# The attention's gate setup is reordered: triangle ahead of identity copies, factors behind one scan, spreads by unit, an own buffer for suffix products, and position stores at other steps

## The chip, the cores and the metric

The kernel runs on one core of one Trainium2 chip. The metric is the device time of one execution in microseconds. TensorE is the matmul engine (PE), VectorE is DVE, ScalarE is ACT, GpSimd is POOL, and SP issues most DMAs. "Unit" below is one step of the attention's main loop.

## The reference

Three stages run one after the other. The first is a gated linear attention over 4 batches, 8 heads, 768 tokens and a head width of 40, with a running maximum m over the gates:

    m_new  = max(f_gate + m, i_gate)
    f_stab = exp(f_gate + m - m_new);  i_stab = exp(i_gate - m_new)
    C = f_stab * C + i_stab * outer(v, k);  n = f_stab * n + i_stab * k
    y = sigmoid(o_gate) * (C q) / max(|n q|, 1)

The second sends each of the 3072 tokens (320 wide) to one of 8 experts by the largest cosine logit; an expert is two matrices with a relu of width 1024, and its result is scaled by the softmax weight. The third is one dense block of width 2048 with x * sigmoid(1.702 x).

## The kernel before

**Attention.** The tokens are cut into 6 chunks of 128. A unit is one (batch, chunk) pair, the batch running fastest, so there are 24 units, and units 0 to 3 are chunk 0. Inside a chunk the products of f_stab between two tokens form a 128 x 128 decay matrix for each head (`pm`). Chunk 0 makes it in `scan0`: matmuls with the identity spread the gates over the partitions (L452) and two VectorE scans turn them into products (L454). Chunks from 1 on make two 64 x 64 blocks by one scan with reset points (`scan`, L430; data `fb`, read back from DRAM where `put_dec` stored it, and `id2`, which is the identity repeated for each head). The block between the halves comes from one matmul (`far_mm`, L439) of `lhsA` and `rhsB`. These are the factors `fa` (products from a token to the end of its first half, made on GpSimd by six doubling steps in `suffix`, L346) and `fb` (products from the start of the second half, the scan `est` of `gates_e`, L330), each split into a rounded part (`fp32r`, a cast on ScalarE) and a rest (a subtraction on GpSimd), and then spread over batches and heads with 0/1 masks (`spread_a`, `spread_b` on ScalarE, with `bmask` and `hmask`).

Around it a unit has the scores (`scores_mm`, L477), wm = scores x decay on VectorE (`scores_w`, L482), wm times values (`pv`, L540), the state of the chunk (`kweigh` L468 on GpSimd, `state` L491, `state_up`, on ScalarE for chunk 0, L508, else on VectorE, L512), the part that comes from earlier chunks (`inter`), the division (`epilogue1`, `epilogue2`, `finish`), and transposes and logits for the experts (`route_t`, `route_l`, L615 to L617, with `enT` from `prep_en`). `vprime` (L461) weighs the values, on GpSimd from unit 1 on.

**Opening.** Six loads bring the gates, three copies of each. Chunk 0's gates go first through `gates_m` (a scan, L302), `gates_x` (L307, L308), `gates_xi` (L312) and two exponentials (L316), then the other 640 tokens through the same, with `gates_xi` on GpSimd. `patterns` (L242 on) needs the triangle `tri`, which GpSimd makes (L218 to L220) behind the copies into `id2` (L211). The suffix products lie in the buffer `mm` of the running maxima, of which `gates_x` and `gates_xi` are readers.

**What sets the order.** Everything in the attention stands under a manual schedule: each engine takes its instructions in the order in which the program writes them, and waits in that order. The main loop is written out by hand with conditions on u; loads for unit u + 3 are issued by SP in unit u. The accumulator `dC` of the state has one buffer, so the state of a unit waits until the update of the unit before has read it.

**Experts.** Eight experts of eight steps each (`s` from 0 to 63, M1 = 8). `rows_and_gates` computes, a few VectorE instructions a step, each token's position and weight; `meta_put` (L1354) then writes for 128 tokens one (token, weight) pair each, 8 bytes, with an indirect DMA from GpSimd. There are 24 such stores; the list `puts` holds their steps. GpSimd also makes a part of the split of the expert weights (L111). The weights of the third stage (`load_c`, L1303) are loaded and converted (`cvt`, L1285 on) beside the experts.

Of the kernel before, what the change touches and what calls it, by code (L numbers as in the profile page):

```python
# [9 lines left out]
F32 = mybir.dt.float32  # L10
# [16 lines left out]
def kernel(ctx, tc, qT_in, kT_in, kvo_in, i_gate, f_gate, expert_emb, tau, w12, wio, out, dbg=None):  # L27
# [116 lines left out]
    with ExitStack() as actx:  # L144
# [65 lines left out]
        for a in range(2):  # L210
            nc.gpsimd.tensor_copy(id2[a * HP:(a + 1) * HP],  # L211
                                  ident[a * HP:(a + 1) * HP, a * HP:(a + 1) * HP].unsqueeze(1).to_broadcast([HP, H, HP]))
        fac = {n: ap1.tile([R3, NCH - CH, HP], F32R, name=n) for n in ("fa", "fb")}
# [58 lines left out]
        est = fd  # L272
        facA = mm[:, 0:(NCH - CH) * HP].rearrange("k (c t) -> k c t", t=HP)
        fz = fg.rearrange("k (c t) -> k c t", t=P)
# [39 lines left out]
        def gates_exp(t, c0, c1):  # L314
            v = rows_of(c0, c1)
            nc.scalar.activation(out=v(t), in_=v(t), func=AF.Exp)  # L316
# [22 lines left out]
        def suffix():  # L339
# [4 lines left out]
            while k < HP:  # L344
                yield
                nc.gpsimd.tensor_tensor(out=facA[:, :, 0:HP - k], in0=facA[:, :, 0:HP - k], in1=facA[:, :, k:HP], op=ALU.mult)  # L346
                k *= 2

        def factor_a(c0, c1):
            cs = slice(c0 - CH, c1 - CH)  # L350
            nc.scalar.copy(fac["fa"][:, cs], facA[:, cs])
            lo = slice(BH, 2 * BH)
            nc.gpsimd.tensor_tensor(out=fac["fa"][lo, cs], in0=facA[lo, cs], in1=fac["fa"][lo, cs].bitcast(F32), op=ALU.subtract)

        def factor_b(c0, c1):

            cs = slice(c0 - CH, c1 - CH)
            late = est[:, c0:c1, HP:P]
            nc.scalar.copy(fac["fb"][:, cs], late)
            lo = slice(2 * BH, R3)  # L360
            nc.gpsimd.tensor_tensor(out=fac["fb"][lo, cs], in0=late[lo], in1=fac["fb"][lo, cs].bitcast(F32), op=ALU.subtract)
            n = c1 - c0
            nc.gpsimd.tensor_tensor(out=late, in0=late, in1=est[:, c0:c1, HP - 1:HP].to_broadcast([R3, n, HP]), op=ALU.mult)
            gd = wk.tile([BH, n, B * G], F32, tag="gd", name="gd", bufs=1)
            gd_t[c0] = gd
            nc.gpsimd.tensor_tensor(out=gd, in0=pairm.unsqueeze(1).to_broadcast([BH, n, B * G]),
                                    in1=est[0:BH, c0:c1, P - 1:P].to_broadcast([BH, n, B * G]), op=ALU.mult)

        def spread_a(c0, c1):
            cs = slice(c0 - CH, c1 - CH)  # L370
            for b in range(B):
                nc.scalar.mul(lhsA[:, b, cs], fac["fa"][:, cs].bitcast(F32), bmask[:, b:b + 1])

# [496 lines left out]
        with tc.manual_schedule():  # L870
# [17 lines left out]
            gates_x(1, NCH)  # L888
            gates_xi(1, NCH)
            gates_exp(fg, 1, NCH)  # L890
            suffix_ops = suffix()
            next(suffix_ops)
            gates_exp(ig, 1, NCH)
            masks()
            nc.sync.dma_start(out=emb, in_=expert_emb)
# [9 lines left out]
            scores_mm(0)  # L905
            gates_pe0()
            scores_w(0)
            vprime(0, nc.vector)
            gates_z(1, NCH)
            put_dec()  # L910
# [5 lines left out]
            for u in range(0, NU - 1):  # L916
# [12 lines left out]
                if ok(u - 1):  # L929
                    epilogue1(u - 1)  # L930
                if u == 1:
                    state(0)
                    scores_w(1)
                    state_up(0)
                if u in (2, 3):
                    scores_w(u)
                if u and ok(u + 1):
                    scan(u + 1)
                if u == 1:
                    gates_e(1, NCH)  # L940
                    factor_b(1, NCH)
                if u > 3:
# [3 lines left out]
                if u == 0:  # L946
                    scan(1)
                if ok(u - 1):
                    pv(u - 1)
                    if batch:  # L950
                        route_rank(batch)
                    epilogue2(u - 1)
# [6 lines left out]
                if ok(u + 1):  # L959
                    vprime(u + 1)  # L960
                    if u == 0:
                        for _ in suffix_ops:
                            pass
                    if units[u + 1][1] < CH:
                        kweigh(u + 1)
                rts = {2: [], 3: [0], 4: [1], 5: [2], 6: [3, 4]}.get(u, [u - 2] if ok(u - 2) else [])
                if rts:
# [9 lines left out]
                if u:  # L977
                    state(u)
                if u == 3:
                    prep_en()  # L980
                if len(rts) > 1:
# [18 lines left out]
                if u == 0:  # L1000
                    factor_a(1, NCH)
                    spread_a(1, NCH)
                if u in (1, 2):
                    spread_b(1, NCH, (u - 1) * H // 2, u * H // 2)
                for i in range(0 if u < US else 1 if u < NU - 5 else 2):
                    if pend:
                        scatter(pend.pop(0))
# [89 lines left out]
    with ExitStack() as mctx:  # L1097
# [427 lines left out]
        with tc.manual_schedule():  # L1525
# [33 lines left out]
            meta_ops = rows_and_gates()  # L1559
            puts = [M1 + 5 + i for i in range(M1)] + [2 * M1 + 6 + 2 * i for i in range(NTILE - M1)]  # L1560

# [14 lines left out]
            for e, m, s in steps:  # L1576
# [7 lines left out]
                if 1 <= s < 4:  # L1584
                    prep_x0(0, s - 1)
                for _ in range({2: 2, 3: 2, 4: 1, 5: 2, 6: 2}.get(s, int(6 < s < 13))):
                    next(meta_ops, None)
# [134 lines left out]
```

## Time and profile before

| | us |
|---|---|
| median of 3 runs (lowest to highest) | 746.87 (744.79 to 747.55) |
| the profiled execution | 746.67 |
| its span, first to last instruction | 744.9 |

| engine | busy, share of the span |
|---|---|
| TensorE | 97% |
| TensorE weight loads | 90% |
| VectorE | 69% |
| ScalarE | 49% |
| GpSimd | 32% |

The attention fills about the first 180 us. In the timeline each line gives the start, the duration, the engine, the line of the program and the tiles (out<-in); in brackets stands how long the engine idled just before and what ended it. Several instructions of one kind in a row are merged (x6), and the duration then covers them all. A line of the windows gives the stretch, its length, the busy us of PE, PEld, DVE, ACT and POOL (with the count of instructions), TensorE's granted clock as a share of 2.4 GHz, the busy share of the DMA engines and GB/s. The mean granted clock of TensorE over the span is 0.991 of 2.4 GHz.

### The profile page before, as it was taken

Reading aid. Unit: us, or ns where it says so; the run is one execution under the profiler, and the core shown is the slowest. Engines: PE = TensorE matmul, PEld = TensorE weight load, DVE = VectorE, ACT = ScalarE, POOL = GpSimd, SP = SyncE. Lnnn points to the kernel's source line nnn. Section 1 sums busy time; section 2 is a strip of 40 time slices with the busy share of each in tenths; the row PEclk is TensorE's granted clock in tenths of the full one; section 3 lists DMA queues with packets and bytes.
Section 4 is the critical chain, followed back from the end, with each engine's and each line's share of the span. In section 5 each row is a group of like instructions: output and inputs, shape, how many; then the busy total and the mean of one; then the engine's idle time right before and its main releaser. Section 6 shows DMA issues by size and latency. Waiting matters only on the chain.

```text
span 744.9 us, 13413 instructions
## 1 busy us (share of the span) xinstructions
PE 719.1 (97%) x4767; PEld 672.5 (90%) x4767; DVE 515.2 (69%) x1080; ACT 367.1 (49%) x855; POOL 237.9 (32%) x355
## 2 busy tenths in 40 slices
PE   7899999999999999999999999999999999999994
PEld 5899999988989899999999989888889999889994
DVE  8668999996699799999967755545545544445542
ACT  3465466545666556676645433433333333334442
POOL 6555677776224434545310003003003003002011
PEclk9899999999999999999999999999999999999998
DMA  5688888833775966777722212202201201101000
GB/s 168 183 260 268 241 243 247 263 123 107 245 273 145 214 210 191 203 196 244 227 81 72 39 37 57 63 1 58 64 1 46 54 1 43 38 0 53 6 19 18
DMA packets 70106, 93.14 MB, mean 125 GB/s; under 512 B 31858, under 2 KB 56530, under 8 KB 70034
## 3 DMA queue, kind: packets, MB, share of 16 engines
q1 hardware_dynamic: 66818, 84.05, 38.8%
q0 software_dynamic: 3072, 7.89, 3.1%
q8 instruction: 38, 0.62, 0.4%
q10 hardware_dynamic: 144, 0.30, 0.1%
q14 instruction: 34, 0.28, 0.1%
HBM read 71.11 MB, written 17.18 MB: 119 GB/s over the span
## 4 chain that ended last, share of the span: by engine, by line
issue 43%; PE 16%; DVE 6%; POOL 5%; DMA 3%; ACT 1%; POOLq 0%; SPq 0%; ACTq 0%; DVEq 0%
PE acc L1221 8%; PE hp L139 7%; POOL out_dram L1266 3%; DMA c<-in_wio_dram 2%; POOL xr L1377 2%; DVE hs L1195 1%; DVE w L122 1%; PE xt L1145 1%; DVE w L112 1%; DMA xr<-y 1%; DVE ex L1287 1%; DVE xl L1147 1%; DVE ex L1292 1%; DVE wout L122 0%; DVE fr L1290 0%
## 5 line engine op out<-in xcount | busy, mean ns | idle before, releaser
L1221 PE MATMUL acc<-wout,hhl 128*128 128x320 f32 x1152 | 187.3, 309 | 0.0
L1221 PEld LDWEIGHTS acc<-wout,hhl 128*128 128x128 f32 x1152 | 175.9, 188 | 7.8 <-DVE o L1248 0.2
L1206 DVE TENSOR_TENSOR sg<-hp,sg 128x512 f32<-128x512 f32 (+1 forms) x112 | 68.9, 615 | 93.4 <-ACT sg L1205 85.8
L139 PE MATMUL hp<-xh,win 128*128 128x512 f32 (+1 forms) x560 | 131.0, 364 | 0.0
L1266 POOL DMA_INDIRECT out_dram<-o,tokd x24 | 24.0, 1002 | 312.7 <-ACT o L1250 309.0
L1205 ACT ACTIVATE sg<-hp 128x512 f32<-128x512 f32 (+1 forms) x112 | 60.4, 539 | 125.0 <-PE hp L139 124.5
L1208 DVE TENSOR_TENSOR hhl<-sg,hhl 128x512 fp32r<-128x512 f32 (+1 forms) x112 | 71.4, 637 | 70.3 <-ACT hhl L1207 69.8
L1221 PE MATMUL acc<-w,hs 128*128 128x320 f32 x636 | 105.0, 310 | 2.7 <-ACT hs L1194 1.4
L139 PEld LDWEIGHTS hp<-xh,win 128*128 128x128 f32 x560 | 93.9, 188 | 11.5 <-ACT xh L1416 0.2
L1207 ACT CAST hhl<-sg 128x512 fp32r<-128x512 f32 (+1 forms) x112 | 62.7, 560 | 80.1 <-DVE sg L1206 77.1
L1221 PEld LDWEIGHTS acc<-w,hs 128*128 128x128 f32 x636 | 96.6, 188 | 5.5 <-DVE hs L1195 2.0
L139 PE MATMUL hp<-xl,win 128*128 128x512 f32 (+1 forms) x336 | 85.7, 363 | 0.0
L111 POOL TENSOR_TENSOR w<-r,w 128x256 fp32r<-128x256 f32 x58 | 49.5, 853 | 102.5 <-ACT w L106 78.9
L139 PEld LDWEIGHTS hp<-xl,win 128*128 128x128 f32 x336 | 58.9, 189 | 10.9 <-DVE xl L1417 0.2
L139 PE MATMUL hp<-xh,w 128*128 128x440 f32 (+6 forms) x320 | 66.8, 338 | 0.0
L139 PEld LDWEIGHTS hp<-xh,w 128*128 128x128 f32 x320 | 51.4, 189 | 1.7
L477 PE MATMUL sp<-qT,kblk 120*128 120x128 f32 x384 | 48.8, 282 | 0.2 <-DVE wm L482 0.2
L1194 ACT ACTIVATE hs<-hp 128x440 fp32r<-128x440 f32 (+6 forms) x64 | 30.2, 471 | 34.8 <-PE hp L139 32.0
L477 PEld LDWEIGHTS sp<-qT,kblk 120*128 120x128 f32 x384 | 46.5, 198 | 0.9 <-issue 0.5
L540 PE MATMUL op<-vp_in,wm 128*128 128x96 f32 (+1 forms) x368 | 43.6, 272 | 0.0
L540 PEld LDWEIGHTS op<-vp_in,wm 128*128 128x128 f32 x368 | 42.9, 192 | 0.0
L139 PE MATMUL hp<-xl,w 128*128 128x440 f32 (+6 forms) x192 | 42.9, 331 | 0.0
(323 smaller groups left out, 1128.6 us busy)
## 6 DMA issues: line engine op xcount, KB each, us to landing
r<-in_w_dram SPq DMA_DIRECT2D x32, 704.0 KB
kvo<-in_kvo_dram SPq DMA_DIRECT2D x24, 480.0 KB
c<-in_wio_dram SPq DMA_DIRECT2D x16, 704.0 KB
fb<-dec SPq DMA_DIRECT2D x40, 128.0 KB
rows<-zt SPq DMA_DIRECT2D x8, 640.0 KB
qT<-in_qT_dram SPq DMA_DIRECT2D x24, 180.0 KB
xr<-y SPq DMA_DIRECT2D x5, 640.0 KB
kblk<-in_kT_dram SPq DMA_DIRECT2D x48, 60.0 KB
```

The lines of the kernel that those rows point to most:

```text
L111: eng.tensor_tensor(out=t[:, 3 * P:5 * P].rearrange("p (c f) -> p c f", c=2), in0=r1[:, 0:2], in1=hif[:, 0:2], op=ALU.subtract)
L139: nc.tensor.matmul(hp, a, b, start=(i == 0), stop=(i == len(seq) - 1))
L477: nc.tensor.matmul(sp[:, h - hs.start], kblk[u % NLD][0:KR, h // 3, h % 3, :], qT[u][0:KR, h // 3, :], start=True, stop=True)
L540: nc.tensor.matmul(ops[:, h * NW:h * NW + n], wm[u][:, h], vp_in[u % NLD][:, h * DV:h * DV + n], start=True, stop=True)
L1194: nc.scalar.activation(out=hh, in_=hp, func=AF.Relu)
L1205: nc.scalar.activation(out=sg, in_=hp, func=AF.Sigmoid, scale=1.702)
L1206: nc.vector.tensor_tensor(out=g, in0=hp, in1=sg, op=ALU.mult)
L1207: nc.scalar.copy(hh, g)
L1208: nc.vector.tensor_tensor(out=hl, in0=g, in1=hh.bitcast(F32), op=ALU.subtract)
L1221: nc.tensor.matmul(acc_t[blk][i], hl if j == 2 else hh, w[:, DM:2 * DM] if j == 1 else w[:, 0:DM], start=(first and j == 0), stop=(last an ...
L1266: sc = nc.gpsimd.indirect_dma_start(out=out, out_offset=bass.IndirectOffsetOnAxis(ap=tokd[:, ti:ti + 1], axis=0), in_=o[:, i], in_offset=None)
L1377: eng.tensor_tensor(out=xr_t[blk], in0=xr_t[blk], in1=gated[:, t0:t0 + n].unsqueeze(2).to_broadcast([P, n, 3 * P]), op=ALU.mult)
```

## The change

- The identity copies into `id2` go from GpSimd to ScalarE, and GpSimd's next work behind the buffers' clearing is the triangle.
- `facA`, the buffer of the suffix products, is a tile of its own instead of a part of `mm`.
- `gates_xi` of chunks 1 to 5 (GpSimd) stands behind the first step of `suffix` (its memset and copy); their second exponential stands behind `gates_pe0`, the masks behind `vprime(0)`.
- `gates_e`, the scan of est, goes from unit 1 to unit 0, behind the scan of unit 1. Both casts (`fa` and `fb`) stand behind it in `factor_hi`, at the end of unit 0. The lo parts (`factor_b`, `factor_a`, GpSimd) go to unit 1, behind `vprime` and `kweigh` of unit 2.
- `spread_a` spreads one batch a unit, in units 2 to 5, instead of all four in unit 0.
- `prep_en` goes from the end of unit 3 to its front, ahead of `scan(4)`.
- The position stores go from steps 13 to 20 and then 22, 24, ... 52 to steps 11 to 15 and then 16, 18, ... 52; the last two steps of `rows_and_gates` ahead of them move from steps 11 and 12 to 9 and 10.

```diff
@@ setup
-            nc.gpsimd.tensor_copy(id2[a * HP:(a + 1) * HP],
-                                  ident[a * HP:(a + 1) * HP, a * HP:(a + 1) * HP].unsqueeze(1).to_broadcast([HP, H, HP]))
+            nc.scalar.copy(id2[a * HP:(a + 1) * HP],
+                           ident[a * HP:(a + 1) * HP, a * HP:(a + 1) * HP].unsqueeze(1).to_broadcast([HP, H, HP]))
...
-        facA = mm[:, 0:(NCH - CH) * HP].rearrange("k (c t) -> k c t", t=HP)
+        facA = ap1.tile([R3, NCH - CH, HP], F32, name="facA")
@@ factors
+        def factor_hi(c0, c1):
+            cs = slice(c0 - CH, c1 - CH)
+            nc.scalar.copy(fac["fb"][:, cs], est[:, c0:c1, HP:P])
+            nc.scalar.copy(fac["fa"][:, cs], facA[:, cs])
...
-            nc.scalar.copy(fac["fa"][:, cs], facA[:, cs])
...
-            nc.scalar.copy(fac["fb"][:, cs], late)
...
-        def spread_a(c0, c1):
+        def spread_a(c0, c1, b):
             cs = slice(c0 - CH, c1 - CH)
-            for b in range(B):
-                nc.scalar.mul(lhsA[:, b, cs], fac["fa"][:, cs].bitcast(F32), bmask[:, b:b + 1])
+            nc.scalar.mul(lhsA[:, b, cs], fac["fa"][:, cs].bitcast(F32), bmask[:, b:b + 1])
@@ ahead of the loop
-            gates_xi(1, NCH)
             gates_exp(fg, 1, NCH)
             suffix_ops = suffix()
             next(suffix_ops)
-            gates_exp(ig, 1, NCH)
-            masks()
+            gates_xi(1, NCH)
...
             gates_pe0()
+            gates_exp(ig, 1, NCH)
             scores_w(0)
             vprime(0, nc.vector)
+            masks()
@@ in the loop
+                if u == 3:
+                    prep_en()
...
-                if u == 1:
-                    gates_e(1, NCH)
-                    factor_b(1, NCH)
...
                 if u == 0:
                     scan(1)
+                    gates_e(1, NCH)
...
                     if units[u + 1][1] < CH:
                         kweigh(u + 1)
+                    if u == 1:
+                        factor_b(1, NCH)
+                        factor_a(1, NCH)
...
-                if u == 3:
-                    prep_en()
...
                 if u == 0:
-                    factor_a(1, NCH)
-                    spread_a(1, NCH)
+                    factor_hi(1, NCH)
                 if u in (1, 2):
                     spread_b(1, NCH, (u - 1) * H // 2, u * H // 2)
+                if 2 <= u < 2 + B:
+                    spread_a(1, NCH, u - 2)
@@ experts
-            puts = [M1 + 5 + i for i in range(M1)] + [2 * M1 + 6 + 2 * i for i in range(NTILE - M1)]
+            puts = [M1 + 3 + i for i in range(5)] + [2 * M1 + 2 * i for i in range(NTILE - 5)]
...
-                for _ in range({2: 2, 3: 2, 4: 1, 5: 2, 6: 2}.get(s, int(6 < s < 13))):
+                for _ in range({2: 2, 3: 2, 4: 1, 5: 2, 6: 2, 9: 2, 10: 2}.get(s, int(6 < s < 9))):
```

## Rows read from the trace of the kernel before

**Rows 1.** Page, busy time of each engine (share of the span, instructions)

```profile
PE 719.1 (97%) x4767; PEld 672.5 (90%) x4767; DVE 515.2 (69%) x1080; ACT 367.1 (49%) x855; POOL 237.9 (32%) x355
```

**Rows 2.** Windows, 70 to 75 us in the attention

```profile
70.00:75.00 5.00, 5.00 (x49) 5.00 (x48) 4.92 (x13) 2.65 (x9) 3.83 (x4) 1.00 0.93 307
```

**Rows 3.** Timeline of VectorE (start, duration), wm of units 0, 2, 5 and 21

```profile
16.37 1.23 DVE L482 TENSOR_TENSOR wm<-sp,pmb 128x1024 f32<-128x1024 f32 x1
...
31.89 1.23 DVE L482 TENSOR_TENSOR wm<-sp,pmb 128x1024 f32<-128x1024 f32 x1 [3.34 <-PE sp L477]
...
53.51 1.21 DVE L482 TENSOR_TENSOR wm<-sp,pmb 128x1024 f32<-128x1024 f32 x1
...
155.06 1.20 DVE L482 TENSOR_TENSOR wm<-sp,pmb 128x1024 f32<-128x1024 f32 x1
```

**Rows 4.** Windows of 1 us, around the fall and the rise of TensorE's clock

```profile
25.00:26.00 1.00, 0.00 (x0) 0.00 (x0) 1.00 (x1) 1.00 (x4) 0.00 (x0) 0.83 0.68 168
...
32.00:33.00 1.00, 1.00 (x9) 1.00 (x8) 1.00 (x1) 0.00 (x0) 0.72 (x1) 0.76 0.66 180
```

**Rows 5.** Timeline, all engines, 14 to 29 us: factors, state of unit 1

```profile
14.46 0.44 POOL L342 COPY mm<-fg 96x315 f32<-96x315 f32 x1 [0.61 <-DMA qT<-in_qT_dram]
...
17.72 4.75 POOL L346 TENSOR_TENSOR mm<-mm 96x315 f32<-96x315 f32 x6
...
22.51 0.46 ACT L351 CAST fa<-mm 96x320 fp32r<-96x320 f32 x1 [3.20 <-POOL mm L346]
...
24.14 1.92 ACT L372 ACTIVATE lhsA<-fa,bmask 96x320 fp32r<-96x320 f32 x4 [1.17 <-POOL fa L353]
24.65 1.46 DVE L330 TENSOR_TENSOR_SCAN fd<-fg,fd 96x640 f32<-96x640 f32 x1
...
25.96 0.84 ACT L508 ACTIVATE Cst<-dC,mask 120x123 f32<-120x123 f32 x3
...
26.95 1.42 PE L491 MATMUL dC<-vp_in,kw 128*120 128x123 f32 x6 [2.84 <-ACT Cst L508]
...
28.16 3.69 PE L477 MATMUL sp<-qT,kblk 120*128 120x128 f32 x16
```

**Rows 6.** Timeline, all engines, 5 to 14 us: the opening

```profile
5.99 0.26 DVE L242 CAST tri<-tri 128x128 bf16<-128x128 f32 x1 [1.94 <-POOL tri L220]
...
6.84 0.40 DVE L302 TENSOR_TENSOR_SCAN mm<-fg,ig 32x128 f32<-32x128 f32 x1
...
10.95 0.82 DVE L307 TENSOR_TENSOR fg<-fg,mm 96x640 f32<-96x640 f32 x1
11.00 1.95 POOL L312 TENSOR_TENSOR ig<-ig,mm 96x640 f32<-96x640 f32 x1 [3.07 <-DVE mm L302]
...
11.80 1.82 DVE L308 TENSOR_TENSOR fg<-fg,mm 96x640 f32<-96x640 f32 x1
...
13.95 2.32 DVE L454 TENSOR_TENSOR_SCAN pmb<-f,ident_h 128x512 f32<-128x512 f32 x2
```

**Rows 7.** Windows, the first 4.5 us

```profile
0.00:4.50 4.50, 2.09 (x3) 1.05 (x4) 2.82 (x13) 1.49 (x2) 3.85 (x9) 1.00 0.52 141
```

**Rows 8.** Timeline of GpSimd, values of unit 3

```profile
32.03 0.72 POOL L461 TENSOR_TENSOR vp_in<-kvo,ei_tok 128x320 f32<-128x320 f32 x1 [1.39 <-DMA kvo<-in_kvo_dram]
```

**Rows 9.** Timeline of GpSimd, values of unit 6

```profile
52.41 1.70 POOL L461 TENSOR_TENSOR vp_in<-kvo,ei_tok 128x320 f32<-128x320 f32 x1
```

**Rows 10.** Timeline of TensorE, the first logits

```profile
43.76 0.49 PE L615 MATMUL r<-enT,xT 128*128 128x128 f32 x2 [0.95 <-ACT enT L408]
```

**Rows 11.** Windows, then timeline, 235 to 260 us: position stores, a weight load

```profile
235.00:240.00 5.00, 5.00 (x32) 4.63 (x31) 4.91 (x9) 2.72 (x7) 2.79 (x4) 1.00 0.64 67
...
240.73 1.03 POOL L1354 DMA_INDIRECT meta<-metat,pos_i  x1 [0.15 <-issue]
...
256.25 0.53 DVE L1285 TENSOR_SCALAR mt<-c 128x704 int32<-128x704 int32 x1 [3.08 <-DMA c<-in_wio_dram]
...
257.59 2.02 PE L1221 MATMUL acc<-w,hs 128*128 128x320 f32 x12 [1.38 <-ACT hs L1194]
```


## The prediction

> **What bounds the kernel now.** The busy line of the page comes first: TensorE 97%, its weight loads 90%, VectorE 69% [rows 1]. That is a mean over stages, so a stretch of the attention is read next: from 70 to 75 us the weight loads fill 5.00 of 5 us and VectorE 4.92 [rows 2]. In the settled attention TensorE issues without a gap; a microsecond by which TensorE's order starts earlier should therefore reach the end. Whether it starts late is read from the product wm = scores x decay, one instruction a unit on VectorE [rows 3]. From unit 5 to unit 21 the starts lie (155.06 - 53.51) / 16 = 6.35 us apart. From unit 0 to unit 5 they need 37.14 us, where five such units are 31.75. So about 5.4 us are lost in the first units, beside what is lost ahead of unit 0. One-microsecond windows and the timeline show the hole: TensorE idles 2.84 us ahead of unit 1's state at 26.95, so from 24.11 on [rows 5]; the granted clock falls at about 25.66 (a mean of 0.83 between the levels 1 and 0.5, that is 2.4 and 1.2 GHz) and is back at about 32.5 (0.76) [rows 4].
>
> Who made TensorE wait is read backwards in the timeline [rows 5]. The state of unit 1 needs the accumulator that ScalarE's update of unit 0 empties, at 25.96. ScalarE stood before it in the cast of fa (3.20 us idle, waiting for GpSimd's suffix products, which ran 17.72 to 22.47) and in four spreads of 1.92 us (1.17 idle). The scores of unit 2 begin at 28.16 and take 3.69 us at the low clock.
>
> **Part 1, the opening.** VectorE idles 1.94 us for the triangle, which waits behind the identity copies on GpSimd [rows 6]. With the copies on ScalarE this goes, and what is next is the gate data. The six gate loads are 6 x 98,304 B = 0.59 MB; the queues had moved 141 GB/s x 4.5 us = 0.63 MB by 4.5 us [rows 7], and the first scan would start at 6.84 - 1.94 = 4.9. I take the whole 1.94 (bounds 0 and 1.94). The copies lie in ScalarE's idle time (1.49 busy of 4.5 us [rows 7]); without that cover they would cost at most the 1.94 again.
>
> The second gate subtraction took 1.82 us, its twin in front of it, of the same shape, 0.82; only GpSimd's subtraction for the other gate (1.95 us) ran beside the second throughout [rows 6]. The change moves that one behind the copy for the suffix, and the copy needs the exponential, so the two no longer meet: 1.00 us less (bounds 0 and 1.00). The masks, moved away, stood for the 0.33 us between the subtraction's end at 13.62 and the scan at 13.95. Together scan 0, and wm of unit 0 behind it, come 3.27 us earlier: 16.37 becomes 13.1. The masks then cost about 0.5 behind unit 0's values, so the store of the decays goes out some 2.7 us earlier.
>
> **Part 2, GpSimd and ScalarE.** The copy for the suffix started at 14.46 [rows 5]; 2.94 earlier is 11.5, its end 12.0, the moved subtraction (1.95 at most) ends at 13.9. That is now in front of kweigh and vprime, two products of about 0.72 [rows 8]: 15.35. Six suffix products in 4.75 end at 20.1. A new meeting must be paid: the scan of est (1.46 us, both inputs in SBUF), which stood alone at 24.65, now runs on VectorE behind scan 1, at about 18.5 to 19.9, beside these products. The price of such a meeting, by rows, is 1.82 - 0.82 = 1.00 on VectorE or 1.70 - 0.72 = 0.98 on GpSimd [rows 6, 8, 9]; I take 1.0 (bounds 0, and six times 0.98 if each product were held): 21.1.
>
> The Trainium skill states in "SBUF — State Buffer", section "Who interferes with whom", that a VectorE instruction with two SBUF inputs and a GpSimd instruction that reads SBUF block each other wholly, whichever starts second. By that rule est's scan would hold GpSimd up to its full 1.46, and the sum below would be 0.5 us poorer; the trace agrees in kind, with about 1.0 in both rows just given.
>
> Behind the suffix ScalarE casts fa (0.46); the cast of fb lies in the wait. What is queued behind that wait is the state update of unit 0 and the copy of its numerator; TensorE waits for the first. It starts at 21.6 for 25.96: 4.4 us earlier. TensorE's state of unit 1 and the scores of unit 2 follow by the same 4.4. If the clock stays up over the gap that is left, these scores need 1.95 us (their length at the high clock, as 3.69 at half is 1.85 to 1.95) for 3.69: 1.7 more. Wm of unit 2 comes at about 31.89 - 6.1 = 25.8.
>
> The lo parts of the factors now stand behind vprime and kweigh of unit 2 on GpSimd: three products more, 2.2 us, and four spreads at 0.48 behind them end near 27.3. ScalarE's next state update begins there; TensorE comes to the state that needs it only after scores, decay broadcasts and values of unit 2, near 30. This costs nothing, and 1:1 beyond about 2.5 us of delay. The four spreads of fa, 1.92 in one piece, become one of 0.48 in each of units 2 to 5, ahead of a copy that TensorE reads much later; ScalarE has room (2.65 busy of 5 us [rows 2]): 0, bounds 0 and 1.9.
>
> **Part 3, the embedding's transposes.** TensorE waited 0.95 us for their copies right before the first logits [rows 10]. Moved ahead of unit 3's scan, they are ready long before: 0.95 less (bounds 0 and 0.95; they now wait for VectorE's normalising of the embedding, which ends about a microsecond ahead of them).
>
> **Part 4, the position stores.** A window with few other transfers, 235 to 240 us, has the DMA engines 0.64 busy at 67 GB/s; at the rate of rows 2 (307 GB/s for 0.93) 67 would take 0.20, so some 0.44 x 5 = 2.2 us went to the two stores in flight, about 1.1 each [rows 2, 11]. A weight load had four stores beside it in its flight (the first is shown, at 240.73; they follow every 2 to 4 us); VectorE waited 3.08 us for it and TensorE then 1.38 [rows 11]. With steps 16 and 18 alone there are two fewer. Bounds 0 and 1.38; I take 0.5, since one late operand can replace the other. The two small vector instructions pulled two steps ahead are the same work: 0, bounds 0.4 either way.
>
> **Sum.** 6.1 + 0.95 + 0.5 = 7.55 us against the profiled execution's 746.67 (span 744.9, 1.8 around it): 739.1. That execution lies 0.2 under the median of the runs shown, 746.87; in that measure the forecast is 739.3.
>
> **Rivals.** First, the clock falls again: TensorE still idles some 1.2 us there, in place of the 2.84 in which the clock fell [rows 4, 5]. Half of the busy time from 26.95 to 32.5 is 2.8: 742.1. For it: a gap remains at the same place; against it: it is less than half as long. Second, the opening does not shrink (gates later than 4.9, or the 1.82 not due to GpSimd): up to 2.9 less, 742.2. Against it stands the 0.63 MB. Third, the loads become the bound: SP's stream starts only 2.7 earlier, and GpSimd already waited 1.39 us for the values of unit 3 [rows 8]; with DMA 0.93 busy [rows 2] the units could then gain no more than 2.7 + 0.5: 743.7. Against it: the settled units load three units ahead and no engine waits there. Fourth, the gain is given back where VectorE is as full as TensorE, or in the experts' stage: 746.7.
>
> The fifth ends on the other side: GpSimd's chain. If each suffix product were held by 0.98 beside VectorE, they would end at 20.1 + 5.9 = 26.0, the cast at 26.5, the state update after 25.96, and the lo parts, spreads and next update follow some 1.4 us later than before, with the clock low as before: 748.1. It decides from the suffix's end at 25.5. Against it: the products ran beside VectorE before, at 4.75 for six [rows 5].
>
> **How the numbers follow.** Forecast 0.48; clock 0.17; opening 0.13; loads 0.10; given back 0.06; GpSimd's chain 0.06. About 0.5% (3.7 us) is what a measurement of this kernel can tell from no change, so faster means under 743.1: nearly all of the forecast, 0.12 of the clock, 0.10 of the opening, 0.04 of the loads: 0.73. Slower by as much is a worse fifth case: 0.05; the rest 0.22. The low end takes the unpaid meeting (1.0), the stores' full 1.38 and some of the first units' other losses: 735.8; the high end the rivals up to the loads: 744.0.
>
> **What would show it.** The first gate scan near 4.9; the second subtraction near 0.82; the suffix's end near 21; the state update of unit 0 near 21.6; wm of units 0, 2 and 5 near 13.1, 25.8 and 46.5; no window at clock 0.5 between 20 and 33; no wait for enT; VectorE's wait for the weight load halved. Wrong would be: wm of unit 5 early by less than 3 us, or early there and not at unit 21.

## The result, and the profile after

The changed kernel takes 738.15 us (median of 4 runs, 736.86 to 739.55) against 745.83 us for the kernel before beside it (4 runs): ratio 0.9896, 95% interval 0.9862 to 0.993, so 0.7 to 1.4% faster. The forecast was 739.3 us, and 735.8 to 744.0 holds the time. The sum was nearly right; two of its terms were not, and their errors cancel, so that the total came out this close is in part luck. The rest of this document is about that.

The busy line of the page hardly moves against [rows 1]: the same work lies in a shorter span (737.9 us; this execution took 739.55).

```profile
PE 714.6 (97%) x4767; PEld 669.6 (91%) x4767; DVE 515.3 (70%) x1080; ACT 368.3 (50%) x857; POOL 237.6 (32%) x353
```

The opening and the factors, in the timeline of the changed kernel (its lines are numbered 2 to 4 higher than before's from `scan` on):

```profile
4.24 0.35 DVE L242 CAST tri<-tri 128x128 bf16<-128x128 f32 x1 [0.18 <-POOL tri L220]
5.17 0.40 DVE L302 TENSOR_TENSOR_SCAN mm<-fg,ig 32x128 f32<-32x128 f32 x1
...
10.16 0.82 DVE L308 TENSOR_TENSOR fg<-fg,mm 96x640 f32<-96x640 f32 x1
...
12.23 1.31 POOL L312 TENSOR_TENSOR ig<-ig,mm 96x640 f32<-96x640 f32 x1
13.33 1.22 DVE L484 TENSOR_TENSOR wm<-sp,pmb 128x1024 f32<-128x1024 f32 x1
...
14.88 5.85 POOL L346 TENSOR_TENSOR facA<-facA 96x315 f32<-96x315 f32 x6
...
18.94 1.46 DVE L330 TENSOR_TENSOR_SCAN fd<-fg,fd 96x640 f32<-96x640 f32 x1
...
20.43 0.46 ACT L351 CAST fb<-fd 96x320 fp32r<-96x320 f32 x1 [1.92 <-DVE fd L330]
20.80 0.45 ACT L352 CAST fa<-facA 96x320 fp32r<-96x320 f32 x1
21.16 0.86 ACT L510 ACTIVATE Cst<-dC,mask 120x123 f32<-120x123 f32 x3
...
22.16 0.80 PE L493 MATMUL dC<-vp_in,kw 128*120 128x123 f32 x6 [0.19 <-POOL vp_in L463]
22.80 1.99 PE L479 MATMUL sp<-qT,kblk 120*128 120x128 f32 x16
24.82 1.23 DVE L484 TENSOR_TENSOR wm<-sp,pmb 128x1024 f32<-128x1024 f32 x1
```

The wait for the triangle is 0.18 us for 1.94 [rows 6], the second subtraction takes 0.82 for 1.82, the update of unit 0's state starts at 21.16 for 25.96, TensorE's idle time ahead of unit 1's state is 0.19 for 2.84, and the scores of unit 2 take 1.99 us for 3.69 [rows 5]. The windows in which the clock fell and rose [rows 4] show full clock:

```profile
25.00:26.00 1.00, 1.00 (x12) 1.00 (x11) 1.00 (x2) 0.45 (x1) 0.92 (x2) 1.00 0.31 100
32.00:33.00 1.00, 1.00 (x11) 0.98 (x10) 1.00 (x1) 1.00 (x5) 1.00 (x3) 1.00 0.91 338
```

The window around the stores [rows 11] is not to be compared at the same time, since the changed kernel is some 4 us further on there. At the same place of the program, 231 to 236 us, its DMA engines are 0.76 busy at 48 GB/s, for 0.64 at 67 before: this window shows no relief. The load's flight does (run 2).

Where the time came from is read best in one row per place: the start (us) of wm of some units, of the 1st, 19th and 23rd relu of the experts (`hs`), and of the last output store, in the profiled executions. "Changed again" is run 8 below, "stores only" run 2, "opening, factors undone" run 10, "weights early" run 9, "three edits" run 12. The lead is the time by which a mark comes earlier than before.

| | before | changed | changed again | stores only | opening, factors undone | weights early | three edits |
|---|---|---|---|---|---|---|---|
| wm unit 0 | 16.37 | 13.33 | 13.33 | 16.49 | 16.36 | 13.22 | 13.33 |
| unit 2 | 31.89 | 24.82 | 25.40 | 31.12 | 31.21 | 24.71 | 24.81 |
| unit 5 | 53.51 | 46.47 | 46.98 | 52.60 | 51.85 | 45.76 | 45.85 |
| unit 11 | 92.73 | 85.31 | 85.79 | 91.80 | 91.07 | 85.10 | 85.19 |
| unit 12 | 98.54 | 93.14 | 93.84 | 97.49 | 96.77 | 90.80 | 91.25 |
| unit 23 | 167.69 | 159.79 | 163.73 | 166.38 | 165.69 | 159.87 | 159.69 |
| 1st relu | 192.06 | 188.07 | 188.60 | 191.66 | 190.43 | 184.40 | 184.17 |
| 19th relu | 248.65 | 244.44 | 245.11 | 248.39 | 247.98 | 242.06 | 240.54 |
| 23rd relu | 267.57 | 259.90 | 260.59 | 263.88 | 263.47 | 257.52 | 256.28 |
| last store | 737.05 | 729.98 | 731.05 | 733.84 | 733.64 | 727.94 | 727.19 |

The lead of the changed kernel is 7.04 us at unit 5 and 7.42 at unit 11. It is 5.40 at unit 12: one step gave back 2.0 us. It is 4.0 to 4.2 at the experts' start and 7.7 at the 23rd relu, so the stretch with the position stores brought 3.5 us, seven times the 0.5 forecast; 2.7 of them are left at the 31st (run 2).

A mark of one execution is not exact. Unit 5 lies at 45.76 to 46.98 in the five profiles with the changed attention (the changed kernel, runs 1, 3, 8 and 9), and at 53.51 and 52.60 in the two with the old one (before, run 2). The lead of 7.90 at unit 23, of which 3.9 us are lost up to the first relu, belongs to this one execution: run 8 has 3.96 and 3.46 there, and run 1 starts the experts 6.49 ahead.

The step from unit 11 to 12 shows what ended it. First before, then after: ScalarE's first split of an expert's weights (L106) stands for the load (L97, issued at 85.98 and at 80.46) to land.

```profile
92.73 1.20 DVE L482 TENSOR_TENSOR wm<-sp,pmb 128x1024 f32<-128x1024 f32 x1
...
93.04 0.51 ACT L106 CAST w<-r 128x384 fp32r<-128x384 f32 x1 [2.55 <-DMA r<-in_w_dram]
...
98.54 1.21 DVE L482 TENSOR_TENSOR wm<-sp,pmb 128x1024 f32<-128x1024 f32 x1
```

```profile
80.46 0.31 SPq L97 DMA_DIRECT2D r<-in_w_dram  x1
...
85.31 1.20 DVE L484 TENSOR_TENSOR wm<-sp,pmb 128x1024 f32<-128x1024 f32 x1
...
87.30 0.37 SPq L97 DMA_DIRECT2D r<-in_w_dram  x1
87.31 0.51 ACT L106 CAST w<-r 128x384 fp32r<-128x384 f32 x1 [4.24 <-issue]
...
93.14 1.20 DVE L484 TENSOR_TENSOR wm<-sp,pmb 128x1024 f32<-128x1024 f32 x1
```

The wait grew from 2.55 to 4.24 us: the load was issued 5.5 us earlier and landed 5.7 us earlier, TensorE's order 7.4. (The profile names "issue" in the second case; the buffer's next load and the split start in the same 0.01 us, and the repeated runs name the DMA.) Behind the split stand VectorE's split (L111, which VectorE awaits for 1.34 us) and ScalarE's other copies of that unit.

Over all profiles the step follows this wait. It takes 7.74 to 8.09 us in the seven with a wait of 4.14 to 4.47 (the changed kernel, runs 1, 3, 6, 7, 8 and 11), 6.76 with 3.16 (run 4), 5.81 with 2.55 (before) and 5.69 to 6.06 in the five with 0.66 or none (runs 2, 5, 9, 10 and 12). So some 2 us of the wait cost nothing here, and what is beyond them is paid about in full.

### The profile page after: what moved, and what is told of

The parts are those of the page before. It is cut to its first block, busy times and chain, and to the rows that moved or that the text cites. A ratio compares the mean times of both kernels' runs of the same rounds, so it can differ in the third digit from the quotient of the medians.

```text
span 737.9 us, 13402 instructions
## 1 busy us (share of the span) xinstructions
PE 714.6 (97%) x4767; PEld 669.6 (91%) x4767; DVE 515.3 (70%) x1080; ACT 368.3 (50%) x857; POOL 237.6 (32%) x353
## 2 busy tenths in 40 slices
DMA packets 70106, 93.14 MB, mean 126 GB/s; under 512 B 31858, under 2 KB 56530, under 8 KB 70034
## 4 chain that ended last, share of the span: by engine, by line
issue 43%; PE 24%; POOL 5%; DVE 2%; DMA 1%; POOLq 0%; ACT 0%; SPq 0%
PE acc L1225 12%; PE hp L139 11%; POOL out_dram L1270 3%; POOL xr L1381 2%; PE xt L1149 1%; DMA xr<-y 1%; DVE w L122 0%; POOL gap L1272 0%; DVE xl L1151 0%; DVE w L112 0%; DVE hs L1199 0%; DVE fr L1294 0%; PE xt L1165 0%; POOLq L1721 0%; DVE ex L1291 0%
## 5 line engine op out<-in xcount | busy, mean ns | idle before, releaser
L111 POOL TENSOR_TENSOR w<-r,w 128x256 fp32r<-128x256 f32 x58 | 49.5, 853 | 102.9 <-ACT w L106 78.4
L479 PE MATMUL sp<-qT,kblk 120*128 120x128 f32 x384 | 47.1, 276 | 0.2 <-DVE wm L484 0.2
L479 PEld LDWEIGHTS sp<-qT,kblk 120*128 120x128 f32 x384 | 44.8, 192 | 0.9 <-issue 0.5
```

Source lines behind the costliest of these rows:

```text
L111: eng.tensor_tensor(out=t[:, 3 * P:5 * P].rearrange("p (c f) -> p c f", c=2), in0=r1[:, 0:2], in1=hif[:, 0:2], op=ALU.subtract)
L479: nc.tensor.matmul(sp[:, h - hs.start], kblk[u % NLD][0:KR, h // 3, h % 3, :], qT[u][0:KR, h // 3, :], start=True, stop=True)
```

## Experiments

Each is timed in five rounds beside the kernel before; runs 1 to 4, 5 to 8 and 9 to 12 shared a chip and its runs of the kernel before (745.89, 747.36 and 746.43 us).

**1. The old store steps in the changed kernel.**

```diff
-puts = [M1 + 3 + i for i in range(5)] + [2 * M1 + 2 * i for i in range(NTILE - 5)]
+puts = [M1 + 5 + i for i in range(M1)] + [2 * M1 + 6 + 2 * i for i in range(NTILE - M1)]
```

> The changed kernel with the position stores and the two vector instructions ahead of them at their steps of before; the attention keeps its changes. Theory A (the stores lie in the flight of a weight load and delay it): VectorE's wait for that load near expert step 20 comes back at about 3 us, and the time rises by 2 to 3 us over the changed kernel. Theory B (the forecast's size: one late operand replaces the other): the time rises by 0.5 us or less.

739.53 us, ratio 0.9922 (0.9899 to 0.9946): by ratio 1.9 us over the changed kernel, nearer to theory A, with intervals that overlap. The wait for the third stage's weights is back:

```profile
249.24 0.85 ACT L1288 ACTIVATE fr<-c 128x704 f32<-128x704 uint32 x1 [3.56 <-DMA c<-in_wio_dram]
249.24 0.53 DVE L1289 TENSOR_SCALAR mt<-c 128x704 int32<-128x704 int32 x1 [2.53 <-DMA c<-in_wio_dram]
```

**2. The new store steps alone, in the kernel before.** (The reverse of that diff.)

> The kernel before with the new store steps alone. Theory A: the 3.1 us wait of VectorE for the weight load goes, and the time falls by 2 to 3 us under the kernel before (about 0.35%). Theory B: it falls by 0.5 us or less. If A holds here and in the run with the old steps, the attention's edits are worth only 4 to 5 us at the end, though they are worth 7.9 at the last unit.

744.11 us, ratio 0.9976 (0.9957 to 0.9996): 1.8 us by the stores alone (0.3 to 3.2 by the interval, so the times do not rule out the bound of 1.38). No engine waits for `c` at this place any more; in the changed kernel ScalarE still does, and VectorE does not:

```profile
248.98 0.86 ACT L1288 ACTIVATE fr<-c 128x704 f32<-128x704 uint32 x1 [1.05 <-DMA c<-in_wio_dram]
```

The load in question was 14.3 us in flight before (issued at 241.96), 13.8 in run 1 (at 235.44) and 11.6 in the changed kernel (at 237.39). From the 19th to the 23rd relu this run takes 15.49 us, where before took 18.92, the changed kernel 15.46 and run 1 18.37. Some of that is given back: from the 23rd to the 31st relu the kernels with new steps take 27.15 us (changed) and 27.16 (this one), those with old steps 26.40 (before) and 26.37 (run 1). These 0.8 us are not idle time of TensorE. Over both stretches, from the 19th to the 31st relu, the twelve profiles with new steps take 42.61 to 42.72 us and the two with old ones 45.32 (before) and 44.74 (run 1): 2.0 to 2.7 us by the trace, and steadier than the times. TensorE is idle in that stretch for 2.09 us before and 1.53 in run 1, and not at all in run 2 and the changed kernel.

**3. The low parts of the first four early hidden tiles on VectorE.**

```diff
-nc.scalar.activation(out=hf, in_=hp, func=AF.Relu)
-nc.gpsimd.tensor_tensor(out=hl, in0=hf, in1=hh.bitcast(F32), op=ALU.subtract)
+nc.vector.scalar_tensor_tensor(out=hl, in0=hp, scalar=0.0, in1=hh.bitcast(F32), op0=ALU.max, op1=ALU.subtract)
```

> The changed kernel, but the low part of the first four early relu tiles is made on VectorE from the accumulator, behind the ordering of the experts, in place of ScalarE's second relu and GpSimd's subtraction. Theory C (between attention and experts the changed kernel gives back time because VectorE's ordering chain now runs beside GpSimd's four subtractions and is stretched by them): the chain from the copy of the counts to the last value takes 2.6 us instead of 4.3, TensorE's 1.9 us wait for it goes, and the experts start 1.5 to 2 us earlier; the end moves by as much, or by less where loads bind. Rival: the chain is long whatever GpSimd does, the four more subtractions on VectorE come later, and the time stays or rises by up to 0.6 us.

737.3 us, ratio 0.9898 (0.9869 to 0.9926): not to be told from the changed kernel's 0.9896. In the profiled execution of the changed kernel VectorE's ordering of the experts ran slowly beside GpSimd (L828, below, under hardware), and TensorE waited 1.88 us for its result. Here the chain takes 2.61 us, as theory C has it, and that wait is gone. But run 1, which has the changed kernel's code there, did not meet it either (3.02 us, no wait), and both have the first relu at 185.57; so it is a matter of the single execution.

**4. The opening undone.**

```diff
-nc.scalar.copy(id2[...], ident[...])
+nc.gpsimd.tensor_copy(id2[...], ident[...])
...
+gates_xi(1, NCH)                 # ahead of the exponential again
 gates_exp(fg, 1, NCH)
```

> The changed kernel with the opening as before: identity copies on GpSimd ahead of the triangle, GpSimd's gate subtraction ahead of the exponential, the second exponential and the masks at their old places; the factor moves, the transposes and the stores stay. Theory D (the opening is in the chain to the first state update): the second subtraction takes 1.82 us again, wm of unit 0 starts at about 16.4, the suffix products end about 3 us later, and wm of unit 5 and the end move by 2 to 3 us. Rival: behind the opening another wait (loads of unit 3, ScalarE) ends last, and less than 1 us is lost at unit 5.

739.52 us, ratio 0.9923 (0.9901 to 0.9944). Wm of unit 0 is at 16.36 again, the wait for the triangle 1.93 and the second subtraction 1.82 us. At unit 5 the loss is 2.35 us (48.82); at unit 12, 1.25 (94.39), since ScalarE then waits 3.16 us for the first weights instead of 4.24. By ratio the time is 2.0 us over the changed kernel's, with intervals that overlap.

**5. The factors' moves undone.**

```diff
-factor_hi(1, NCH)
+factor_a(1, NCH)
+for b in range(B):
+    spread_a(1, NCH, b)
...
+if u == 1:
+    gates_e(1, NCH)
+    factor_b(1, NCH)
```

> The changed kernel with the factors as before: scan of est in unit 1, the cast of fa, its rest and all four spreads in unit 0, the cast of fb and its rest in unit 1; opening, transposes and stores stay changed. Theory E (ScalarE's queue in front of the first state update is the hole): suffix end near 19.8, then cast, rest and 1.9 us of spreads, so the update starts near 23.2 in place of 21.2, TensorE idles over 2 us and the clock may fall; wm of unit 5 comes 2 us later with the clock up, 4 with it down, and the end 1.5 to 4 us later. Rival (the opening did most of it): less than 1 us.

739.08 us, ratio 0.9887 (0.9844 to 0.9929). In place the loss is plain. The spreads stand ahead of the update again, TensorE idles 2.12 us and its scores of unit 2 take 2.96:

```profile
21.27 1.92 ACT L371 ACTIVATE lhsA<-fa,bmask 96x320 fp32r<-96x320 f32 x4 [1.17 <-POOL fa L353]
...
23.09 0.84 ACT L507 ACTIVATE Cst<-dC,mask 120x123 f32<-120x123 f32 x3
...
24.08 1.42 PE L490 MATMUL dC<-vp_in,kw 128*120 128x123 f32 x6 [2.12 <-ACT Cst L507]
...
25.29 2.96 PE L476 MATMUL sp<-qT,kblk 120*128 120x128 f32 x16
```

Its windows: TensorE did nothing from 22 to 24 us, and the granted clock is at 0.50, that is 1.2 GHz, from 24 us on:

```profile
22.00:23.00 1.00, 0.00 (x0) 0.00 (x0) 1.00 (x2) 1.00 (x3) 0.00 (x0) 1.00 0.35 123
...
25.00:26.00 1.00, 1.00 (x7) 1.00 (x6) 0.78 (x3) 0.83 (x3) 0.92 (x2) 0.50 0.36 110
```

Wm of unit 5 is at 48.94, 2.47 later than in the changed kernel, and ScalarE waits 0.50 us for the first weights: at unit 12 the loss is 0.73 (93.87), and in the time none can be told.

**6. The embedding's transposes at their old place.**

```diff
 if u:
     state(u)
+if u == 3:
+    prep_en()
```

> The changed kernel with the embedding's transposes back at the end of unit 3. Theory F: TensorE waits about 0.95 us again for their copies at the first logits, and the end comes up to 1 us later. Rival: in the changed kernel TensorE waits there for the first token tile anyway (1.1 us before its transposes), so the wait for the copies is hidden in it or follows it with less than 0.3 us; no difference can be measured.

739.5 us, ratio 0.9895 (0.9851 to 0.9939). TensorE's weight load waits 0.37 us for `enT`, after 1.31 for the token tile; the clock then is at 0.50 from 37 to 40 us, and unit 4's scores take 3.02 us:

```profile
34.77 0.33 PE L586 MATMUL pr<-ident,x 128*128 128x128 f32 x1 [1.31 <-POOL x L580]
...
36.59 0.39 PEld L617 LDWEIGHTS r<-enT,xT 128*128 128x128 f32 x2 [0.37 <-ACT enT L410]
...
37.92 3.02 PE L479 MATMUL sp<-qT,kblk 120*128 120x128 f32 x16
```

Unit 5 is 1.9 us late (48.37); the time is the same.

**7. Only GpSimd's subtraction ahead of the exponential again.**

```diff
+gates_xi(1, NCH)
 gates_exp(fg, 1, NCH)
...
-gates_xi(1, NCH)
```

> The changed kernel with GpSimd's gate subtraction alone put back ahead of the exponential. Theory G (two instructions that read two tiles each from SBUF hold each other): VectorE's second subtraction takes 1.8 us again in place of 0.82, GpSimd's 1.95 in place of 1.31, and wm of unit 0 starts 1.0 us later; kweigh and vprime are then free of it, so the suffix's end moves by 0 to +0.5, and the end of the kernel by under 0.5 us. Rival: the second subtraction was long for a reason of its own and stays at 0.82 or was helped by the buffer.

738.49 us, ratio 0.9883 (0.984 to 0.9925). The meeting is back, as it was before, with GpSimd's subtraction at 1.95 us for 1.31, and with it 0.89 us at unit 0 (14.22). Unit 5 is 0.10 late (46.57), which the 45.76 to 46.98 of the changed attention do not tell from nothing:

```profile
9.24 1.95 POOL L312 TENSOR_TENSOR ig<-ig,mm 96x640 f32<-96x640 f32 x1 [3.07 <-DVE mm L302]
10.05 1.82 DVE L308 TENSOR_TENSOR fg<-fg,mm 96x640 f32<-96x640 f32 x1
```

**8. The changed kernel once more.**

> The changed kernel once more. If the 3 us between the last relu of the early tiles and the first expert step in its first profile belong to the change (VectorE's ordering beside GpSimd's subtractions), they show again: 12.5 us between the two. If they are an accident of one execution, the distance is 9.4 us as in the kernel before, the span lies near 735.5, and the 3.1 us wait for the weight load stays away all the same.

739.66 us, ratio 0.9891 (0.9848 to 0.9934). Its lead at unit 23 is 3.96 us, where the first profile of it had 7.90; by the first relu both have 3.5 to 4.0. One execution lost, mostly in the units with a routing batch, what the other lost in the transition; a mark as late as unit 23 is good to some 3 us in one profile. The distance that the expectation names (12.54 us in the first profile and 9.41 before, from the first of the early tiles' relus to the experts' first) is 10.68 here, between the two cases, and the span is 738.9, not 735.5; the wait of 3.1 us stays away.

The times of runs 4 to 7 tell no single edit of the attention from none, while unit 5 comes 1.9 to 2.5 us late in the traces of runs 4, 5 and 6. Runs 9 and 10 were made to decide it.

**9. The first expert's weights one unit earlier, in the changed kernel.**

```diff
-WLOAD = [W0 - 1, W0] + ...
+WLOAD = [W0 - 2, W0] + ...
-if u == W0 - 2:
+if u == W0 - 3:
     first()
-if u == W0 - 1:
+if u == W0 - 2:
     ids[0] = nc.values_load(first_i, ...)
```

> The changed kernel with the choice of the first expert (L752 to L761), its number's way into SyncE's register and the load of its first weights (L97) one unit earlier, at unit 8 instead of 9; the splits on ScalarE stay where they are. Theory (what the attention gains at its opening is given back to this load): in the changed kernel the load was issued at 80.46 us, ScalarE stood 4.2 us in front of the first split (L106), and the step from unit 11's to unit 12's masked scores took 7.83 us, where the kernel before took 5.81 and the kernel before with the new stores 5.69. With the load a unit earlier that wait is under 1 us, the step is 5.6 to 6.0 us, unit 23's masked scores come 1.5 to 2.2 us earlier than in the changed kernel with the same steps elsewhere, and the time is 736.5 to 738.0. Rival (the loads together set the pace of the attention): the wait goes from this place and comes back on the values or keys of the next units, the steps from unit 12 to 23 grow by what step 11 loses, and the time is 739 to 740.

737.51 us, ratio 0.9867 (0.9837 to 0.9897). Wm of units 11 and 12, and the split between them, with no wait:

```profile
72.71 0.37 SPq L97 DMA_DIRECT2D r<-in_w_dram  x1
...
82.75 0.52 ACT L106 CAST w<-r 128x384 fp32r<-128x384 f32 x1
...
85.10 1.20 DVE L484 TENSOR_TENSOR wm<-sp,pmb 128x1024 f32<-128x1024 f32 x1
...
90.80 1.20 DVE L484 TENSOR_TENSOR wm<-sp,pmb 128x1024 f32<-128x1024 f32 x1
```

The step is 5.70 us for 7.83, and the time lies where the theory put it, 2.1 us under run 11, which kept the wait (6 runs each on the same chip; their intervals overlap). Eight of the twelve runs of run 9 and run 12, both with the load early, lie under the lowest of run 11's six (737.58). Unit 23, forecast 1.5 to 2.2 us earlier, is only level with the first profile of the changed kernel, 3.9 us ahead of run 8's. The rival is right in part: from unit 12 to 23 this run takes 69.07 us, for 66.65 and 69.89 in the two profiles of the changed kernel. Over all profiles, from unit 11 to the first relu, the seven with a wait over 4 us take 100.09 to 102.81 us (the middle one 100.49), run 4 with its 3.16 takes 98.39, and the six with at most 2.55 take 98.98 to 99.86 (middle 99.3). So of the 2.1 us that the step loses some 1.2 are left at the experts.

**10. Opening and factors both undone.** (The diffs of runs 4 and 5 together.)

> The changed kernel with its opening (id copies on GpSimd, second subtraction ahead) and its factor moves (one scan position, casts, spreads) both undone; embedding's transposes and position stores as changed. Theory (each edit is real, and one undone alone costs 2.3 to 2.5 us at unit 5, of which the wait for the first expert's weights takes up to 2 back): both undone cost 5 to 6 us at unit 5 (masked scores of unit 5 at 51.5 to 52.6, where the changed kernel has 46.5), the clock falls to 0.5 for some us between 20 and 33 us, ScalarE's wait for the weights is under 2 us, and the time is 742.5 to 744.1. Rival (the two single undoings came out at no difference, so the attention's edits do nothing that reaches the end, and the gain is the stores' and an accident): 739 to 740.5 again.

743.13 us, ratio 0.995 (0.993 to 0.9971). Unit 5 is at 51.85, and a window at 28 us has the low clock:

```profile
26.00:27.00 1.00, 0.08 (x1) 0.11 (x2) 0.09 (x1) 1.00 (x5) 0.00 (x0) 1.00 0.49 144
28.00:29.00 1.00, 1.00 (x7) 1.00 (x6) 0.46 (x3) 0.91 (x2) 0.84 (x3) 0.50 0.85 209
```

With the first weights late, opening and factors together bring 743.13 - 739.59 (run 11) = 3.5 us; with these weights early, 743.13 - 737.51 = 5.6, against 6.1 forecast for the two. (The interval of this run is clear of run 9's and touches run 11's.) With the opening alone (run 5) the order comes up to the wait of unit 12 and loses nothing to it, the step being 5.70 us; with the factors alone (run 4) it loses 1.06, with both some 2. So undoing one shows little in the time.

**11. Unit 3's values loaded ahead of the decays.**

```diff
+load_v(3)
 put_dec()
```

> The changed kernel with the load of unit 3's keys and values for the state (L200, one issue) put ahead of the store of the decays and the loads that follow it on SyncE's queue (L283, six of L292). In the changed kernel GpSimd stood 3.75 us for these values at 31.38 us, and unit 1's finish and unit 0's tile for the router stood behind it (TensorE waited 1.14 us for x at 35.21). Theory (that wait is the bound of units 3 to 5 now): GpSimd's wait under 1 us, TensorE's wait for x gone, masked scores of unit 5 0.8 to 1.5 us earlier (45.0 to 45.7); at the end all of it is taken by the wait for the first expert's weights, which grows by as much, so the time stays at 739 to 740. Rival (the wait costs nothing where it stands): unit 5 at 46.3 to 46.6, time the same; then it is told by unit 5 alone.

739.59 us, ratio 0.9899 (0.9866 to 0.9932). GpSimd's wait for unit 3's values is gone (0.50 us are left, for unit 4's), TensorE's for the token tile too, and unit 5 is at 46.03, between the two forecasts; but run 9, without this edit, had neither wait and 45.76. So the waits differ from execution to execution, and unit 5 settles nothing here. ScalarE still waits 4.14 us for the first weights, and the time is as the theory says.

**12. Runs 3, 9 and 11 in one kernel.**

> The changed kernel with the two edits above (first weights a unit earlier, unit 3's values ahead of the decays) and the low parts of the first four early hidden tiles made on VectorE from PSUM in one instruction each, without ScalarE's second relu and GpSimd's subtraction. Theory: what unit 5 gains is no longer taken back at unit 12; unit 23's masked scores at 156.0 to 158.0, time 735.0 to 737.0, faster than the changed kernel by 2.5 to 4 us. Rival (the loads set the pace): 738.5 to 740.

736.77 us, ratio 0.9865 (0.9834 to 0.9896): the lowest of all, by ratio 2.3 us under the changed kernel's first timing and 1.9 under its second, for the 2.5 to 4 forecast; the intervals overlap, so it is the best version only by its median. Unit 23 is at 159.69, where the theory had 156 to 158.

## Why the prediction was right, step by step

- **The opening** (13.1 for wm of unit 0; measured 13.33), **the factors** (state update at 21.6; 21.16), the clock that stays up (unit 2 at 25.8; 24.82) and unit 5 (46.5; 46.47) went as written. The first scan was at 5.17, not 4.9. The first rival (the clock falls again) did not come. TensorE's gap was 0.19 us here, not 1.2. In run 8 it was 1.78 at the same place, and the clock stayed at 1.00 in every window of 1 us from 18 to 34. Unit 21, the last of the signs, was 7.42 us early here and 3.96 in run 8.
- **The second subtraction** went to 0.82 as forecast, and run 7 brings the 1.82 back. The reading behind it was loose: GpSimd's subtraction started at 11.00 and so lay beside the first one too (10.95 to 11.77 [rows 6]), which kept its 0.82 us.
- **The meeting of est's scan with the suffix products** was priced at 1.0. Six products take 5.85 us beside the scan; in run 5, where est's scan is elsewhere, they take 4.74: 1.11. All of it lies in the sixth product, which starts at 19.10, 0.16 us into the scan, and takes 1.63 us, for 0.53 in run 5. The Trainium skill ("SBUF — State Buffer", section "Who interferes with whom") would have the one that starts second wait until the other ends. That would be 1.30 us here, and 1.10 of them show.
- **The transposes' 0.95**: the wait for `enT` went, but in the profiled execution 1.14 us for the token tile stood in its place. GpSimd had stood 3.75 us for unit 3's values (1.39 before [rows 8]), with unit 1's finish behind it:

```profile
31.38 0.72 POOL L463 TENSOR_TENSOR vp_in<-kvo,ei_tok 128x320 f32<-128x320 f32 x1 [3.75 <-DMA kvo<-in_kvo_dram]
...
35.21 0.33 PE L586 MATMUL pr<-ident,x 128*128 128x128 f32 x1 [1.14 <-POOL x L580]
```

  Run 10 against run 2 gives 0.75 us at unit 5 and 0.20 at the last store. Run 2 is itself 0.91 ahead of before at unit 5 with the same attention, so what the transposes are worth at the end stays open. The load rival was right in kind: for these values in a part of the executions, and for the first expert's weights at unit 12. What the prediction held against it, that no engine waits for a load in the settled units, is not so in the trace of before (2.55 us at 93.04).
- **The step that failed** is the sentence that a microsecond by which TensorE's order starts earlier should reach the end, since the attention issues without a gap. It was read from one window [rows 2] and from the distance of units 5 and 21. The step from unit 11 to 12 is in the trace of before with a wait of 2.55 us on it. In the changed kernel the step took 2.0 us back, of which some 1.2 stayed lost up to the experts (run 9). Of the 7.04 us at unit 5 (7.05 forecast), 5.4 were left behind unit 12. In the times Parts 1 and 2 brought 3.5 us of their 6.1, and 5.6 with run 9's load.
- **The mis-sized term** is Part 4: 0.5 us forecast, bounds 0 and 1.38, about 1.8 by medians (run 2) and 2.0 to 2.7 by the trace. I had priced TensorE's one wait behind the late weights. Before has a second one in that stretch, 0.71 us at 272.80 for a relu on VectorE; both, 2.09 us together, are gone in the changed kernel and in run 2. VectorE's wait (3.08 [rows 11]) went wholly, not by half.
- So the gain of 7.7 us beside the 7.55 forecast is two wrong terms in one sum: opening and factors at 3.5 for 6.1, the stores at 1.8 for 0.5. The 2.4 us that are left are the transposes and the errors of the medians, which no run here parts.

## What to carry to other kernels

Before a gain at the start of a long loop is carried to its end, list the distance of every pass, not the mean and one window: one pass with a load on its path can take back part of what comes earlier. When undoing single edits shows nothing, undo two, and remove the wait that may hide them. A late operand costs what everything behind it on its engine loses, not the first TensorE wait that shows.

## Hardware, not expected

Some small VectorE instructions took several times as long beside a GpSimd one. In the ordering chain of the changed kernel's profile, beside 2.81 us of GpSimd (the reductions of that chain, L843, kept their 0.20 to 0.22 us there):

```profile
176.28 2.81 POOL L828 TENSOR_TENSOR he<-hf,he 128x256 fp32r<-128x256 f32 x4 [1.59 <-ACT hf L827]
...
177.15 0.65 DVE L858 TENSOR_TENSOR spare<-spare 128x64 f32<-128x64 f32 x1
```

In run 1 the same GpSimd work started behind that chain, and the instruction took 0.22:

```profile
175.86 0.22 DVE L858 TENSOR_TENSOR spare<-spare 128x64 f32<-128x64 f32 x1
...
176.93 2.83 POOL L828 TENSOR_TENSOR he<-hf,he 128x256 fp32r<-128x256 f32 x4 [1.64 <-ACT hf L827]
```

The chain from the copy of the counts (L849) to the last cast's end (L868) took 4.45 us in the one and 3.02 in the other. In run 8 a 128x32 product (L643) took 0.66 us beside GpSimd's `kw`, 0.19 in the first profile, and wm of the unit with it came 8.39 us behind the last instead of 7.14 (the step ahead of it took 5.48 for 6.11). Which of the two happens changes from execution to execution; that it makes part of the scatter of the times is likely, but not shown.

The clock also fell after short waits: in run 6 TensorE idled 1.31 us to 34.77, its weight load 0.37 to 36.59; it was 0.95 busy from 36 to 37 us, the granted clock was 0.88 there and 0.50 in the three windows after. In the changed kernel, with the 1.14 us alone, it stayed at 1.00.
